# An early small inverse for the first token block of an S4 + GEGLU kernel, with half-size transposes and a new instruction list

## The chip, the cores and the metric

The kernel runs on one core of a Trainium2 chip. The time is device microseconds of one execution; before the change the median of three runs is 804.17 us (801.27 to 805.13). The core has five engines with an instruction stream each: TensorE (PE in the profile, with its weight loads as PEld), VectorE (DVE), ScalarE (ACT), GpSimd (POOL) and SyncE (SP). DMA transfers are issued from the streams of SP, ACT and POOL, and wait there in line with the engine's other instructions.

## What is computed

One sequence of 2048 tokens with 448 channels goes through two residual parts, both with a layer norm whose scale and shift come from a condition vector (adaLN).

```python
mod = silu(c) @ w_mod                       # six rows of 448: sa, ca, ga, sb, cb, gb
h = layernorm(x) * (1 + ca) + sa
K[d, l] = Re( sum_n C[d,n] * exp(dt[d] * A[d,n] * l) * dt[d] * B[d,n] )   # 448 x 2048, n = 256
y = irfft(rfft(h, 4096) * rfft(K, 4096))[:2048] + h * Dskip               # long convolution
x = x + ga * y
h = layernorm(x) * (1 + cb) + sb
x = x + gb * ((gelu(h @ w_gate) * (h @ w_up)) @ w_down)                   # 448 -> 1792 -> 448
```

The convolution is done in fp32, the two wide products of the second part with each fp32 operand split into two fp16 halves ("hi" and "lo").

## The kernel before

**Stage 1, generation and convolution.** The convolution kernel K is made on the chip. For each of 56 sets of eight channels ScalarE computes exponentials (L655, L637), angles go through TensorE (L668) and become sines and cosines on ScalarE (L681, L692, under one table load or another), VectorE multiplies them to tx and ty (L714, L718), and TensorE contracts over n (kgen, L741: 32 columns wide, in four column groups; then L764). Meanwhile the input is normalised and transformed. The transform of length 4096 is split in a stage over 32 and a stage over 128 rows; the results of the first stage go through DRAM and come back with other rows on the partitions. Channels come in three groups of 160, 160 and 128 (`GCH`). A group's transform runs over batches of frequencies: forward (TensorE), product with the input's transform (VectorE), inverse (TensorE), copy out of PSUM, store to `y_d` in DRAM.

**The join of the stages.** The last group's K is ready last, so its transform, `t_fft`, stands between the stages. It has nine batches (`TB`): eight of four frequencies and one of one. A batch is `t.fwd` (L1160), one product over 128 partitions (`t.p0`, L1166) and two over 64 (`t.p1`, L1169), `t.inv` (L1176, weights of 128 columns, all 2048 tokens), `t.z` (the copy out of PSUM, L473 on ACT or L475 on DVE, into one of two buffers "zo" or two "lh") and `t.st` (the store, L1184). PSUM for `t.inv` comes from the pool `fft` with two banks. Then the tokens of the first block (512 of 2048) are read back: `yi.l` (L1246, two per batch), and for the batch of one frequency `yi.d` (L1258, rows straight from zo to yi).

With yi complete, the second inverse stage runs for the first block: `co.mme` (L1356, the 320 channels of groups 0 and 1) can go early, `co.mml` (L1361, the last 128 channels) waits for all of yi. Then come the residual add, the statistics (L1368), the norm (L1403, L1404), the split into hi and lo (`hl`), the transposes `co.ta` (four of hi) and `co.tb` (four of lo, L1419) into one PSUM tile of eight, and the copies `co.ca`, `co.cb` into `ht`. The weights of the gate and up products are loaded and split by `w.hi` (L1297, ACT) and `w.lo` (L1301, DVE). Between these steps TensorE runs 18 "spins" (L1021), two matmuls each, whose result nobody reads.

**Stage 2, GLU.** For each of four blocks: gate and up (`gu2` and `gu`, L1470, L1476), gelu on ACT (L1483), product on DVE (L1490), split, and the product with w_down (L1576). The later blocks' loads and joins run beside it.

**What sets the order.** Nothing is ordered at run time. `PLACE` gives each step (by name and running number) a position in one list, and by a letter the engine or queue where there is a choice (a ScalarE, d VectorE, p POOL, s SP); `Plan.run` calls the steps sorted by that position, and so each engine's stream is written. The framework puts in the waits. Steps named `ev.` close pools of buffers, so that others can open on their memory; what is allocated there waits for the closed ones (`GATE`).

Of the kernel before, what the change touches and what calls it, by code (L numbers as in the profile page):

```python
# [40 lines left out]
    "anc": "106 134 153 161 146 178 189 230 255 295 302 329 320 337 428 447 456 478 486 512 502 561 568 617 660 684 694 687",  # L41
    "ang": "105 119 133 142 143 176 188 199 242 294 301 313 316 328 400 424 449 453 472 496 498 549 567 593 649 658 670 686 "
        "735 737 744 757 758 788 789 863 871 888 891 907 920 921 985 1000 1002 1014 1027 1033 1103 1111 1125 1127 1141 1150 "
        "1160 1172",
    "bn": "52 66 64 65 26 33 28 27 216 221 219 220 138 217 149 140",
    "c.ai": "1243",
    "c.ak": "174",
    "c.au": "17",
    "c.c": "8",
    "c.ea": "18",  # L50
    "c.ih": "1270",
    "c.ld": "6",
    "c.rd": "61",
    "c.t1": "19",
    "co.adde": "1310 1320 1338 1334",
    "co.addl": "1349 1354 1385 1388",
    "co.addx": "1469 1478 1479 1471 1647 1701 1674 1665 1766 1767 1781 1779",
    "co.c2": "1549d 1557d 1550d 1555a 1717d 1731a 1724a 1732d 1854a 1859d 1867a 1866a",
    "co.ca": "1378a 1379d 1414d 1415a",
    "co.cb": "1381a 1383d 1418a 1417a",  # L60
    "co.h0": "1364a 1371a 1400a 1403a",
    "co.h2": "1502d 1545a 1513a 1530d 1709a 1719a 1706a 1722d 1811d 1802a 1852d 1832a",
    "co.l0": "1372 1377 1406 1407",
    "co.l2": "1503 1547 1518 1541 1710 1720 1708 1723 1812 1804 1860 1853",
    "co.mme": "1303 1312 1314 1333",
    "co.mml": "1348 1353 1366 1374",
    "co.mmx": "1450 1473 1474 1451 1621 1695 1658 1620 1765 1746 1778 1777",
    "co.n": "1363 1369 1392 1397",
    "co.nx": "1492 1519 1508 1529 1707 1716 1704 1721 1810 1790 1793 1784",
    "co.rc": "1362 1368 1391 1393",  # L70
    "co.rcx": "1487 1703 1783",
    "co.rt": "1350 1355 1386 1390",
    "co.rtx": "1483 1702 1782",
    "co.t2": "1516 1556 1533 1551 1713 1725 1712 1727 1813 1847 1862 1855",
    "co.ta": "1365 1375 1408 1410",
    "co.tb": "1376 1382 1409 1411",
    "cos": "743 762 763 774 785 795 805 876 897 900 906 918 946 945 996 1009 1023 1040 1041 1048 1115 1121 1134 1155 1168 "
        "1169 1191 1207",
    "cos2": "118 135 154 162 152 187 193 238 260 297 304 335 323 340 436 448 459 483 487 516 507 564 573 621 675 685 701 693",
    "d.hi": "1524 1504 1544 1454 1486 1559 1468",  # L80
    "d.ld": "1511 1495 1532 1441 1481 1548 1456",
    "d.lo": "1528 1507 1546 1458 1488 1563 1472",
    "d0": "1",
    "dn": "1564 1565 1575 1576",
    "dn.k0": "1698 1849 1957",
    "dn.k2": "1711 1856 1959",
    "dn.k3": "1718 1861 1962",
    "dn.r": "1566 1568 1589 1578",
    "dn.r1": "1715 1872 1960",
    "dn.r4": "1728 1864 1964",  # L90
    "dn.r5": "1734 1871 1971",
    "dn.r6": "1735 1870",
    "dn.rh": "1965 1973 1977",
    "dn.s0": "1976",
    "dn.s1": "1978",
    "dn.st": "1573 1587 1617 1607 1748 1749 1750 1751 1972 1970 1898 1924 1969 1974 1975",
    "dn0": "1696 1697 1846 1848 1954 1955",
    "dn1": "1699 1850 1956",
    "dn2": "1726 1863 1966",
    "dn3": "1733 1865",  # L100
    "dn3h": "1967 1968",
    "dn4": "1705 1857 1961",
    "dn5": "1700 1851 1958",
    "dn6": "1714 1858 1963",
    "dsk": "34",
    "dt": "23",
    "e.f": "1618 1680 1661 1574 1610 1586 1639",
    "e.hi": "1623 1682 1662 1577 1611 1591 1645",
    "e.ld": "1613 1677 1650 1572 1609 1585 1626",
    "e.lo": "1624 1683 1667 1579 1615 1595 1648",  # L110
    "ev.end": "1229",
    "ev.fp": "691",
    "ev.geg": "1339",
    "ev.ps": "1313",
    "ev.ub": "380",
    "f.fc": "703 704 755 772 791 810 835 866 881 913 927 1003 1022 1034 1058 1083 1104 1124 1156 1173",
    "f.fwd": "729 754 771 797 818 847 868 893 908 935 959 981 993 1020 1039 1063 1084 1109 1126 1147 1179 1190",
    "f.inv": "738 765 786 809 832 857 874 902 923 949 968 991 1010 1032 1057 1069 1097 1123 1131 1161 1203 1215",
    "f.pr": "730 761 778 808 819 848 869 896 912 948 961 989 1005 1026 1042 1064 1089 1112 1128 1151 1181 1198",
    "f.st": "768 821 804 834 865 880 885 931 956 999 997 1006 1038 1078 1079 1094 1113 1143 1166 1201 1211 1222",  # L120
    "f.ut": "692 746 756 784 792 824 845 877 884 916 928 957 982 1004 1024 1035 1077 1085 1107 1132 1157 1174",
    "f.z": "747a 799a 790a 829a 861a 879a 883a 929a 947d 964a 986d 998d 1028a 1047a 1062a 1092d 1106d 1135a 1165a 1185a "
# [1657 lines left out]
```

## Time and profile before

| | before |
|---|---|
| median of three runs | 804.17 us (801.27 to 805.13) |
| profiled execution | 805.04 us |
| its span | 803.2 us |
| granted TensorE clock, mean | 0.987 |
| DMA | 136.72 MB, 170 GB/s over the span |
| chain that ended last | PE 73%, ACT 13%, DMA 5%, DVE 4%, issue 2% |

The span runs from the first to the last instruction. A row of busy time names the line of the kernel, the engine, the operation and the tiles (out<-in), then count, busy time, mean duration in ns and the idle time ahead of the group with what ended it. The chain is followed backwards from the last instruction: at each step to what released it. The profile's lines L... are those of the kernel before; in the changed kernel the same code stands 5 to 36 lines lower.

### The profile page before, as it was taken

The page shows a single profiled execution, that of the slowest core. Times are in us where ns is not written, and L with a number is a line of the kernel's source. Part 1 is how long each engine was busy: PE and PEld are TensorE (multiplying, and loading weights), DVE is VectorE, ACT ScalarE, POOL GpSimd, SP SyncE. Part 2 cuts the span into 40 slices and gives each one's busy share as a digit, 9 for nine tenths or more (in the row PEclk, how much of TensorE's full clock was granted, in tenths as well). Part 3 has the DMA queues.
Part 4 walks back from the last instruction along what each step waited for, and adds up shares of the span by engine and source line. Part 5 has one row for each costly group of instructions (what it writes and reads, how often), then busy time and mean ns, then how long its engine had stood idle before and what let it go on. Part 6 is the DMA issues. An engine that isn't in the chain of part 4 may idle for free.

```text
span 803.2 us, 19013 instructions
## 1 busy us (share of the span) xinstructions
PE 743.2 (93%) x8202; PEld 451.0 (56%) x8202; DVE 597.6 (74%) x896; ACT 456.7 (57%) x592; POOL 9.7 (1%) x25
## 2 busy tenths in 40 slices
PE   2677888999899999989899999999999999999998
PEld 1234444544577777769474445444595446954478
DVE  4889998999899999988667972288773776236462
ACT  3699999899899998951355730043441343113230
POOL 0000000000000000001200000000000000000000
PEclk9989999999999999999999999999999999999999
DMA  8554368898778857989587756246443222012101
GB/s 267 157 151 152 95 178 255 251 277 241 199 218 263 235 166 215 291 294 307 167 256 237 242 182 183 51 145 228 134 93 119 92 93 92 1 58 92 58 10 61
DMA packets 90397, 136.72 MB, mean 170 GB/s; under 512 B 21560, under 2 KB 72056, under 8 KB 90314
## 3 DMA queue, kind: packets, MB, share of 16 engines
q1 hardware_dynamic: 85808, 128.26, 53.3%
q10 hardware_dynamic: 3946, 6.60, 2.4%
q8 instruction: 64, 1.05, 0.5%
q0 software_dynamic: 560, 0.66, 0.3%
q14 instruction: 19, 0.16, 0.1%
HBM read 100.37 MB, written 36.01 MB: 170 GB/s over the span
## 4 chain that ended last, share of the span: by engine, by line
PE 73%; ACT 13%; DMA 5%; DVE 4%; issue 2%; SPq 0%; ACTq 0%; DVEq 0%; POOLq 0%
PE pq L1476 31%; PE pq L1576 9%; PE kg L741 4%; PE pg L668 4%; PE pd L1545 4%; PE pf L1089 4%; ACT my L655 2%; ACT fg L681 2%; PE pq L1470 2%; PE pf L970 2%; PE kg L764 2%; PE pf L1078 2%; ACT fg L692 2%; PE pd L1576 2%; DMA y<-zo 1%
## 5 line engine op out<-in xcount | busy, mean ns | idle before, releaser
L1476 PE MATMUL pq<-ht,wr 128*128 128x512 f16 (+1 forms) x1200 | 249.0, 365 | 1.7 <-DVE ht L475 0.9
L1476 PEld LDWEIGHTS <-wr 128*128 128x128 f16 x1200 | 114.5, 98 | 129.5 <-issue 13.2
L718 DVE TENSOR_TENSOR ty<-my,fg 128x2048 f32<-128x2048 f32 x56 | 127.4, 2285 | 1.0 <-ACT fg L692 0.5
L1483 ACT ACTIVATE ge<-pq 128x512 f32<-128x512 f32 (+1 forms) x60 | 33.8, 566 | 97.2 <-PE pq L1470 61.7
L1502 ACT ACTIVATE hh<-fq 128x1024 f16<-128x1024 f32 (+1 forms) x49 | 46.6, 963 | 72.6 <-DVE fq L1497 40.5
L1490 DVE TENSOR_TENSOR fq<-ge,pq 128x512 f32<-128x512 f32 (+1 forms) x60 | 39.0, 649 | 59.7 <-PE pq L1476 36.2
L1576 PE MATMUL pq<-d,hh 128*128 128x224 f16 x476 | 69.2, 259 | 0.0
L714 DVE TENSOR_TENSOR tx<-mx,fg 128x1024 f32<-128x1024 f32 x56 | 67.8, 1218 | 0.5 <-issue 0.5
L1505 DVE TENSOR_TENSOR hlo<-fq,hh 128x1024 f16<-128x1024 f32 (+1 forms) x49 | 53.7, 1106 | 18.4 <-ACT hh L1502 18.4
L741 PEld LDWEIGHTS kg<-ty,tx 128*32 128x32 f32 x3584 | 55.1, 113 | 20.8 <-issue 9.1
L741 PE MATMUL kg<-ty,tx 128*32 128x64 f32 x3584 | 64.4, 225 | 1.9 <-DVE tx L714 1.5
L1576 PE MATMUL pq<-d,hlo 128*128 128x224 f16 x238 | 61.6, 259 | 0.0
L681 ACT ACTIVATE fg<-pg 128x1024 f32<-128x1024 f32 x56 | 57.4, 1033 | 1.5 <-PE pg L668 1.0
L655 ACT ACTIVATE my<-pg 128x1024 f32<-128x1024 f32 x56 | 55.7, 1032 | 3.3 <-PE pg L650 2.9
L1576 PEld LDWEIGHTS <-hh 128*128 128x128 f16 x560 | 53.9, 98 | 0.6 <-issue 0.2
L1089 PE MATMUL pf<-q,fc 128*128 128x160 f32 x264 | 41.9, 308 | 1.3 <-DVE q L1082 0.9
L668 PEld LDWEIGHTS <-lt 64*128 64x128 bf16 x336 | 19.5, 95 | 42.1 <-issue 28.5
L668 PE MATMUL pg<-ea,lt 64*128 64x512 bf16 x168 | 34.5, 392 | 7.9 <-ACT fg L681 3.6
L1089 PEld LDWEIGHTS pf<-q,fc 128*128 128x128 f32 x264 | 36.5, 190 | 7.2 <-issue 4.4
L1693 ACT ACTIVATE d<-fq 128x896 f16<-128x896 f32 x14 | 13.2, 946 | 43.3 <-PE pd L1545 27.3
L668 PE MATMUL pg<-rd,lt 64*128 64x512 bf16 x168 | 34.0, 385 | 0.0
L668 PE MATMUL pg<-ea,rd 64*128 64x512 bf16 x168 | 34.0, 385 | 0.0
(191 smaller groups left out, 1139.9 us busy)
## 6 DMA issues: line engine op xcount, KB each, us to landing
wr<-w_d SPq DMA_DIRECT2D x21, 896.0 KB
fc<-in_k_fc SPq DMA_DIRECT2D x20, 576.0 KB
u_d<-so SPq DMA_DIRECT2D x32, 224.0 KB
ui<-u_d SPq DMA_DIRECT2D x10, 672.0 KB
fq<-in_wd SPq DMA_DIRECT2D x14, 448.0 KB
w<-in_wgu SPq DMA_DIRECT2D x11, 512.0 KB
us<-uo SPq DMA_DIRECT2D x22, 240.0 KB
q<-us SPq DMA_DIRECT2D x22, 240.0 KB
```

The lines of the kernel that those rows point to most:

```text
L655: A.activation(yb.tile.rearrange("p h (n k) -> p n h k", n=2), pb.tile.rearrange("p (n h k) -> p n h k", n=2, h=2), AF.Exp)
L668: T.matmul(pa[:, nh * 512:nh * 512 + 512], w, x, start=(k == 0), stop=(k == 2))
L681: A.activation(fb.tile[:, 0].rearrange("p x (n k) -> p n x k", n=2), pb.tile.rearrange("p (n x k) -> p n x k", n=2, x=2), AF.Sin, scale=TW ...
L714: V.tensor_mul(tx.tile, xb.tile[:, xm, None, :].to_broadcast([128, 2, 512]), fb.tile[:, :, 0])
L718: V.tensor_mul(ty.tile, yb.tile[:, :, None, :].to_broadcast([128, 2, 2, 512]), fb.tile[:, None, :, 1].to_broadcast([128, 2, 2, 512]))
L741: T.matmul(kg[32 * g:32 * g + 32, 2 * (s % 2) + q, :64], tx[:, r, nh, 4 * q + g], ty[:, 0:4:3, nh, 4 * q + g] if r else ty[:, 1:3, nh, 4 * ...
L1089: T.matmul(pz.tile[:, e % 32 - sl0], fc.tile[:, i, 1 + t], pp.tile[:, t, i], start=(t == 0 and e != 32), stop=(t == 1 and e != 0))
L1476: T.matmul(pb.tile[k][:, ts], wr.tile[:, 4 * lo + t, k, c0:c0 + 128], ht[:, m, ts], start=f % 2 == 0 and i == 0, stop=f % 2 == 1 and i == 9)
L1490: V.tensor_mul(to if half is None else to[:, half:half + 1], *src)
L1502: A.activation(hg.tile[0][:, cb, c], fq.tile[:, c], AF.Copy)
L1505: V.tensor_sub(hg.tile[1][:, cb, c], fq.tile[:, c], hg.tile[0][:, cb, c])
L1576: T.matmul(bank(k)[:, m], x[:, p, q[0], ts], w[:, p, q[1]], start=new and m == 0 and p == 0 and z == 0, skip_group_check=True, stop=i in ( ...
```

## The change

**A small inverse.** The columns of the inverse matrices are permuted so that the rows of a result come in order of token block. `t.i0` computes, from the same products, the inverse for the first block's tokens alone: 32 columns per frequency, the four frequencies of a batch in the four column groups of TensorE (`tile_position`). `t.z0` copies the 128 x 128 result into a buffer of the same two pairs "zo" and "lh", `t.s0` stores it (64 KB) into a new DRAM buffer `yb_d`, and `yi.l` reads the first block from there, two loads for each of the nine batches. `yi.d` is gone. The full `t.inv`, `t.z` and `t.st` stay: blocks 1 to 3 need them.

**Pools.** Products of the last five batches lie in the slots "my". The pool for norm, split and transposed tiles (`w0`) opens once the last batch's forward transform, the first two full inverses and the stores of group 1 are done, and PSUM for `co.mme` on the later token tiles and for the spins (`ev.pq`) once all products are done, not all copies.

**Half tiles.** For the first block, hi and lo are transposed into two PSUM tiles of four, from the pool `pd`; `co.ca` depends on the first four transposes alone.

**Spins.** 6 in place of 18.

**The list.** All of `PLACE` is new, in stage 1 as well, with other choices of engine in places.

```diff
-    spin(18, [EV["ps"], c_ih], Buf("pq"), None, lambda: POOLS["ps"].tile([128, 512], FT, name="pq0"),
+    spin(6, [EV["pq"], c_ih], Buf("pq"), None, lambda: POOLS["ps"].tile([128, 512], FT, name="pq0"),
...
+    perm = np.arange(128).reshape(2, 2, 2, 4, 4).transpose(3, 0, 1, 2, 4).reshape(128)
...
-        fc[:, i, 1] = c1.reshape(128, 128)
-        fc[:, i, 2] = c2.reshape(128, 128)
+        fc[:, i, 1] = c1.reshape(128, 128)[:, perm]
+        fc[:, i, 2] = c2.reshape(128, 128)[:, perm]
...
-    y_d = [dram.tile([32, 2, 64, n], FT, name="y%d" % g) for g, n in enumerate(GCH)]
+    y_d = [dram.tile([32, 128, n], FT, name="y%d" % g) for g, n in enumerate(GCH)]
+    yb_d = dram.tile([32, 2, 2, 2, 4, 128], FT, name="yb_d")
...
+        def inv0():
+            p0.tile = fft.tile([128, 128], FT, name="pf")
+            for t in range(2):
+                for i, (b, k, _) in enumerate(fs):
+                    e = EORD[i0 + i]
+                    r = 32 * (e % 32 - sl0)
+                    T.matmul(p0.tile[r:r + 32], b.tile[:, k, 1 + t, :32], pp.tile[:, t, i],
+                             start=(t == 0 and e != 32), stop=(t == 1 and e != 0), tile_position=(0, r))
+
+        def zout0(e):
+            z0.tile = pq.tile([128, 128], FT, name=z0.tag, bufs=2)
+            cp(e, z0.tile[:32 * ns], p0.tile[:32 * ns])
+
+        def store0(q):
+            QF[q](yb_d[sl0:sl0 + ns].rearrange("s r h g j d -> (s r h g j) d"), z0.tile[:32 * ns])
...
+        t5 = add("t.i0", {"PE": 0.52 if ne > 1 else 0.25}, v, inv0, t4, [p0], fb + [pp])
+        t6 = add("t.z0", {"ACT": 0.2, "DVE": 0.2}, v, zout0, [t5], [z0], [p0])
+        S0[bi] = add("t.s0", {"SP": 0.41, "ACT": 0.4, "POOL": 0.83}, v, store0, [t6], (), [z0], kb=16 * ns)
...
+            def yl(q, s0=s0, ns=ns, g=g):
+                QF[q](y_rows(YI[0].tile, 2)[64 * g + 2 * s0:64 * g + 2 * (s0 + ns)],
+                      yb_d[s0:s0 + ns, :, :, g].rearrange("s r h j d -> (s r) h (j d)"))
+            YL.append(add("yi.l%d" % g, {"SP": 0.68, "ACT": 0.75, "POOL": 0.7}, 58.5 + 0.1 * bi, yl, [S0[bi], t_yi], (),
+                          [YI[0]], kb=16 * ns))
...
-    EV["ps"] = add("ev.ps", {"NONE": 0.0}, 58.9, ev_ps, TZ + MR)
+    EV["pq"] = add("ev.pq", {"NONE": 0.0}, 58.8, ev_pq, TQ)
+    EV["ps"] = add("ev.ps", {"NONE": 0.0}, 58.9, ev_ps, TZ + MR + [EV["pq"]])
+    EV["w0"] = add("ev.w0", {"NONE": 0.0}, 58.8, ev_w0, [YO[1, b] for b in range(NB)] + [TI[0], TI[1], TS[len(TB) - 1]])
...
-            def tr16(k0=None, pt=pt, hl=hl):
-                if not k0:
-                    pt.tile = POOLS["ps"].tile([128, 8, 128], HF, name="pt")
-                for k in range(k0 or 0, 8 if k0 is None else k0 + 4):
-                    T.transpose(pt.tile[:, k], hl.tile[:, 128 * k:128 * k + 128], K2["ih"])
+            pts = [pt, pt if blk else Buf("pd")]
+
+            def tr16(k0=None, pts=pts, hl=hl):
+                b = pts[1 if k0 else 0]
+                n, k0 = (8, 0) if k0 is None else (4, k0)
+                b.tile = POOLS["pd" if n == 4 else "pt"].tile([128, n, 128], HF, name="pd" if n == 4 else "pt")
+                for k in range(n):
+                    T.transpose(b.tile[:, k], hl.tile[:, 128 * (k0 + k):128 * (k0 + k) + 128], K2["ih"])
```

Two lines of the table show its form, those of the spins:

```diff
-    "spin": "1325 1335 1336 1342 1343 1344 1345 1346 1347 1352 1356 1357 1358 1359 1360 1361 1367 1373",
+    "spin": "1312 1320 1321 1332 1333 1376",
```

What it does to the streams is seen at three places. The first is TensorE ahead of the join. Before (L1176 is the full inverse, L1356 the join's early channels, L1021 a spin; the join's last channels, L1361, come after sixteen spin matmuls more):

```order
L1160 MATMUL pf<-ako,my 128x128 x6
L1176 MATMUL pf<-q,fg 128x128 x32
L1356 MATMUL pd<-yi,ai 64x320 x2
L1176 MATMUL pf<-q,fg 128x128 x4
L1176 MATMUL pf<-q,my 128x128 x12
L1356 MATMUL pd<-yi,ai 64x320 x2
L1356 MATMUL pq_5259<-yi,ai 64x320 x2
L1021 LDWEIGHTS idenh
L1021 MATMUL pq_5278<-idenh 128x512
```

Now (L1195 is the small inverse, L1186 the full one, L1381 and L1386 the join's early and last channels, L1447 the transposes), from the last spin matmul ahead of the join on:

```order
L1026 MATMUL pq_5264<-idenh 128x512
L1186 MATMUL pf<-q,fg 128x128 x8
L1381 MATMUL pq_5261<-yi,ai 64x320 x2
L1186 MATMUL pf<-my,fg 128x128 x16
L1386 MATMUL pd<-yi,ai 64x128 x4
L1186 MATMUL pf<-my,fg 128x128 x12
L1186 MATMUL pf<-my 128x128 x4
L1447 LDWEIGHTS hl
```

All full inverses stood ahead of the join, the last two with the early channels between; now three of the later batches stand close ahead of it, two behind it, and the last one ahead of the first GLU matmul. The small inverses stand before all of this, two to eight rows of matmuls each.

The second place is POOL's queue from the first store of the last group on. Before:

```order
L1184 DMA y_69<-zo 128x3x128
L1258 DMA yi<-zo 1x4x128 x2
L1246 DMA yi<-y_69 8x2x512 x2
L1258 DMA yi<-zo 1x4x128 x2
L1246 DMA yi<-y_69 6x2x512
L1246 DMA yi<-y_69 8x2x512
L1258 DMA yi<-zo 1x4x128 x2
L1246 DMA yi<-y_69 8x2x512 x3
```

Now (L1203 is the small store, L1275 the load of the first block, L1210 the full store):

```order
L1203 DMA yb_d<-zo 128x128
L1203 DMA yb_d<-lh 96x128
L1203 DMA yb_d<-lh 32x128
L1203 DMA yb_d<-zo 128x128
L1275 DMA yi<-yb_d 8x2x512
L1275 DMA yi<-yb_d 6x2x512
L1275 DMA yi<-yb_d 8x2x512 x2
L1275 DMA yi<-yb_d 6x2x512
L1203 DMA yb_d<-zo 128x128
L1275 DMA yi<-yb_d 8x2x512 x6
L1210 DMA y_69<-lh 128x4x128
L1210 DMA y_69<-zo 128x4x128 x3
```

The queue had one store and loads; now it has five small stores among the loads, and full stores at its end.

The third place is the start, on ScalarE, from the last step that takes the time step dt to the copy zo for the modulation. Before:

```order
L554 ACTIVATE q<-q,dts__105 112x256
L588 DMA lh_d<-lh 112x1536
L573 ACT_TABLE_LOAD
L573 ACTIVATE q<-q 112x256
L581 ACTIVATE q<-q 112x256
L826 ACTIVATE rows<-pf 128x448
L473 ACTIVATE zo<-pf 128x448
```

Now:

```order
L559 ACTIVATE q<-q,dts__106 112x256
L790 ACTIVATE sig<-c_sb 112x4
L478 ACTIVATE lh<-q 112x2x256 x2
L578 ACT_TABLE_LOAD
L578 ACTIVATE q<-q 112x256
L593 DMA lh_d<-lh 112x1536
L586 ACTIVATE q<-q 112x256
L478 ACTIVATE zo<-pf 128x448
```

Two casts (L478 into lh) that VectorE did stand on ScalarE, the table load and the store come after them, and the copy zo stands ahead of the rows of the modulation.

More of the change, by code (lines that the diff above doesn't have):

```diff
@@ L428, in s4_geglu @@
     V.memset(eps, 1e-5)
-    ph1, ph1b, ph1t, ph1f = (ExitStack() for _ in range(4))
+    ph1, ph1b, ph1t, ph1f, ph1c = (ExitStack() for _ in range(5))
     cst = ph1.enter_context(tc.tile_pool(name="cst", bufs=1))
@@ L437, in s4_geglu @@
     pq = ph1b.enter_context(tc.tile_pool(name="pq", bufs=4, side="right", reuse_waits="tile"))
-    akps = [ph1b.enter_context(tc.tile_pool(name="ak0", bufs=1, side="right"))]
+    akps = [ph1c.enter_context(tc.tile_pool(name="ak0", bufs=1, side="right"))]
     uas, gzs = ExitStack(), ExitStack()
@@ L1031, in s4_geglu @@
     X1, W = {}, {}
-    yv = [y.rearrange("s r (h g j) d -> (s r) g h (j d)", h=2, g=2) for y in y_d]
+    yv = [y.rearrange("s (b r h g j) d -> s b r g h (j d)", b=4, r=2, h=2, g=2) for y in y_d]
     def y_rows(t, c):
```

111 lines of the change are left out of this document (53 added, 58 removed), and 433 rows, old and new, of the table PLACE.

## The prediction

> **What bounds the kernel now.** I read the busy shares first, then busy time by stretch, then the chain that ended last around the change of stage, and last the single groups on it.
>
> ```profile
> PE 743.2 (93%) x8202; PEld 451.0 (56%) x8202; DVE 597.6 (74%) x896; ACT 456.7 (57%) x592; POOL 9.7 (1%) x25
> ```
>
> A share of 93% is a mean over two stages. By stretch (columns: stretch, length, busy PE, PEld, DVE, ACT, POOL, granted clock, DMA share):
>
> ```profile
> 0.00:40.00 40.00, 17.89 (x64) 7.70 (x65) 26.76 (x63) 21.01 (x32) 1.55 (x11) 0.96 0.74 212
> 40.00:361.00 321.00, 291.70 (x5278) 183.21 (x5278) 301.40 (x350) 295.01 (x360) 0.00 (x0) 0.98 0.75 217
> 320.00:361.00 41.00, 36.69 (x863) 28.44 (x863) 38.19 (x39) 31.94 (x38) 0.00 (x0) 1.00 0.92 288
> ...
> 361.00:382.00 21.00, 20.98 (x181) 20.18 (x182) 18.07 (x29) 4.24 (x7) 2.77 (x5) 1.00 0.99 304
> ...
> 404.00:800.00 396.00, 394.61 (x2574) 231.03 (x2573) 235.27 (x419) 129.06 (x182) 0.00 (x0) 1.00 0.39 123
> ```
>
> From 404 to 800 us only TensorE counts (394.6 of 396): nothing there gets shorter without fewer matmuls, and the change leaves that stage's matmuls as they are. From 40 to 361 three engines are each over 90% busy, so their order decides. Between lies the join of the stages, 361 to 404.3, which is a chain (start, length, what):
>
> ```profile
> 357.12 1.10 PE kg L741 x64
> ...
> 361.00 3.14 PE pf L1160 x26
> ...
> 372.99 3.59 PE pf L1176 x32
> ...
> 376.65 0.61 ACT zo L473
> ...
> 377.27 4.17 DMA y<-zo
> ...
> 381.53 0.61 ACT zo L473
> ...
> 382.15 2.50 DMA y<-zo
> ...
> 384.94 0.69 DVE zo L475
> ...
> 385.66 0.41 DVE x L1367
> 386.07 4.22 DMA y<-zo
> ...
> 390.89 2.29 DMA yi<-y
> ...
> 393.95 0.44 PE pd L1361 x4
> ...
> 395.30 4.38 PE pq L1021 x12
> ...
> 400.27 0.97 PE pq L1021 x4
> ...
> 402.80 0.95 ACT wr L1297
> ...
> 404.28 1.80 PE pq L1476 x15
> ```
>
> I call 361.00, the first forward transform of the last group, T0. The last load lands so late that the last group's join (L1361) starts at T0+32.95; the GLU matmuls run from T0+43.3, or T0+42.85 if the four that ran a little earlier are taken off. What stands between the last product (VectorE) and the join is three copies and three stores in a row, because two zo buffers are used over and over:
>
> ```profile
> 379.46 1.39 DVE L1169 TENSOR_TENSOR q<-my,pf 64x512 f32<-64x512 f32 x2
> ...
> 384.94 0.69 DVE L475 COPY zo<-pf 128x512 f32<-128x512 f32 x1 [4.09 <-DMA y<-zo]
> ```
>
> The last product ends at 380.85 = T0+19.85, and a copy then sits 4.09 us behind a store.
>
> **The change, part by part.** (1) *Small inverse.* A transform whose weights are 32 columns wide, four in four column groups, has its like in L741: 64 matmuls of 64 columns in 1.10 us, 17 ns each. With 128 columns 34 ns; the 66 written ones run as two passes (L1160 shows 66 records for 33 written), so 132 × 34 ns = 4.5 us more TensorE. Twelve spins go, 24 matmuls at 0.24 us (0.97 for four) = 5.8 us. These spins filled waiting time, and the small inverse runs while the products bound: I cost both at nothing. Without the column groups running together it would be 132 × 0.121 (3.14/26) = 16 us.
>
> (2) *The products* (VectorE, 0.69 us each) keep their number. Two small copies are put among them and one full copy of the first batch more than before:
>
> ```profile
> L475 DVE COPY zo<-pf 128x128 f32<-128x128 f32 x1 | 0.3, 292 | 0.0
> ```
>
> 2 × 0.29 + about 0.45 = +1.0: last product at T0+20.85.
>
> (3) *From there to the join.* The shortest data path: small inverse 0.5, copy 0.3, issue and landing of the store 0.4 + 2.5, load 2.29 with 0.65 + 0.78 around it (the gaps before and after the load at 390.89): T0+28.3. But TensorE's order puts four spins (1.9), three full inverses (3.59/2 = 1.8 each) and a join matmul group (0.4) behind the last small inverse and ahead of the join: 20.85 + 0.5 + 1.9 + 5.4 + 0.4 = T0+29.1 at the earliest. These inverses also need PSUM banks that copies empty, and copies need buffers that stores empty: nine small and four full copies go through four buffers before, three turns each. A store from the POOL queue, which gets four of the first five small stores, is shown once, and its loads beside it:
>
> ```profile
> y<-zo POOLq DMA_DIRECT2D x1, 192.0 KB, 8.1
> ...
> yi<-y POOLq DMA_DIRECT2D x6, 32.0 KB, 3.4
> ```
>
> At 3.4 us a turn is about 4.4, three turns 13, from the first copy at T0+6 to T0+19: not binding. At 8.1 a turn is 9.2, so T0+33.7, and one inverse more: T0+35.5. I take T0+32: 64 KB is nearer in size to the 32 KB, but the stretch has a DMA share of 0.99. Against 32.95 that is −0.95, with ends −3.85 (T0+29.1) and +2.55 (T0+35.5). The Trainium skill ("DMA: Bandwidth & Descriptors", section on the SWDGE path) gives a POOL transfer as about 2.0 us plus its bytes at 436 GB/s, an estimate of 2.15 us for 64 KB; by that the order of TensorE alone would bind, and the sum would be 2.9 us lower. The trace speaks against it: 192 KB took 8.1 us, where the page makes 2.45.
>
> *Its queues.* The eight tiny DMAs from zo straight to yi go (six on POOL, two on SP), nine small stores come (five on POOL, two each on SP and ScalarE's queue), and the full stores now stand behind the loads. POOL issues 16 DMAs before the join, at up to
>
> ```profile
> 367.10 0.79 POOL L1184 DMA_DIRECT2D y<-zo  x1 [364.79 <-ACT zo L473]
> ```
>
> each, 12.6 us of the 26 from T0+6 on: room enough. But a load that waits on POOL for its store holds the next small store behind it; that is one more reason not to take T0+29.1. On SP the third weight load stands ahead of the last stores where it stood behind them, so the cast that follows it is sooner free.
>
> (4) *From the join to the GLU* it took 42.85 − 32.95 = 9.9 us, most of it statistics, normalisation, transposes. The half tiles let a copy begin after four transposes, not eight; against that the last full inverse, 1.8 us, now stands ahead of the first GLU matmul, in the place where TensorE waits for a weight cast (L1297, 402.80) and a copy until 404.28, about 1.8 us after its transposes; if the copies come sooner, the inverse does not. I take 9.7: −0.2, between −1 and +1.
>
> (5) *Where spins go, the clock may.* In the last column but two:
>
> ```profile
> 395.00:396.00 1.00, 1.00 (x7) 0.43 (x6) 0.84 (x5) 0.29 (x1) 0.00 (x0) 0.73 0.00 0
> 396.00:397.00 1.00, 1.00 (x4) 0.32 (x3) 0.96 (x4) 0.30 (x1) 0.00 (x0) 0.50 0.43 102
> ...
> 398.00:399.00 1.00, 1.00 (x4) 0.42 (x3) 0.96 (x3) 0.35 (x3) 0.00 (x0) 0.56 0.73 299
> 399.00:400.00 1.00, 1.00 (x12) 0.57 (x9) 0.97 (x3) 0.67 (x2) 0.00 (x0) 1.00 1.08 444
> ```
>
> TensorE had stood for 2.6 us before 393.95; 1.3 us later it got half its clock for 3.3 us, which hit only spins. Now the gap between the join and the transposes (5.7 us before, full of spins) holds one join and two inverses, 4 us, so gaps stay near 2 us: cost 0, at most 1.65 (3.3 us at half clock under the first GLU matmuls). The Trainium skill ("TensorE: Matmul & The Clock Gate", Part 1) wants an idle window of about 3.4 us for that; by that rule the cost is 0 as well, but here 2.6 us was enough.
>
> (6) *Phase 1.* At the start one product of the modulation is taken ahead, and both halves of another run in one go:
>
> ```profile
> 15.35 5.55 PE L808 MATMUL pf<-fg,c_sb 112*128 112x448 f32 x8 [15.35 <-DMA fg<-in_w_mod]
> ...
> 26.25 4.87 PE L808 MATMUL pf<-fg,c_sb 112*128 112x448 f32 x8
> ...
> 24.74 0.54 ACT L473 ACTIVATE zo<-pf 128x448 f32<-128x448 f32 x1
> ...
> 33.00 2.86 ACT L655 ACTIVATE my<-pg 128x1024 f32<-128x1024 f32 x3
> ```
>
> The copy zo can move from 24.74 to about 20.8 (a table load, two casts and three small steps ahead of it); then 0.5 + 10.4 gives 31.7 where the second half now ends at 31.1, so the first exponential moves from 33.0 to 33.6: +0.6. Six casts change from VectorE to ScalarE, and two table loads go:
>
> ```profile
> L473 ACT ACTIVATE lh<-q 112x512 bf16<-112x512 f32 x6 | 3.8, 630 | 1.2 <-DVE q L529 1.1
> L573 ACT ACT_TABLE_LOAD x1 | 1.3, 1283 | 5.5 <-DVE q L566 5.5
> ...
> L475 DVE CAST lh<-q 112x512 bf16<-112x512 f32 x10 | 4.2, 425 | 1.0 <-ACT q L554 0.7
> ```
>
> VectorE 6 × 0.425 = −2.6; ScalarE 6 × 0.63 − 2 × 1.28 = +1.2; the other copies that change sides come to −0.5 and +1.2 by the same count. VectorE ends the stage (38.19 of the last 41 us), ScalarE has 26 us idle there against 19.6: I take half of −3.1, and with the start T0 comes 1.0 us earlier. What the new order opens or closes of idle no row shows; a quarter of VectorE's 19.6 us either way is 4.9, so −6 to +5.5.
>
> (7) The stage from 404 on: its first load of block 1 comes later but has tens of microseconds; 0, within 1.
>
> Sum: −1.0 − 0.95 − 0.2 = −2.15. The profiled execution took 805.04 (span 803.2), close to the slowest of the three runs shown; on the median of 804.17 the forecast is 802.0.
>
> **Rivals.** *A, the chain gives all it could.* Stores land in 2.2 to 3.4 us, the join comes at T0+29.1: −1.0 − 3.85 − 0.2 gives 799.1. For it: HW-queue stores of 256 KB took 2.50 beside traffic. Against: 4.17, 4.22 and 8.1 in the same stretch. The skill's price for a POOL transfer leads here.
>
> *B, slower: ScalarE becomes what phase 1 waits for.* It gets 2.4 us more work and keeps copies that wait for TensorE in its own queue:
>
> ```profile
> ACT ke L473 <- PE kg L741: 4.8, 2, 4.0
> ```
>
> Exponentials, angles and cosines stand behind such a copy, TensorE's angle matmuls behind these, VectorE's products behind all. Two more waits of 4.0 us make 802.0 + 8.0 = 810.0; from one and a half on the kernel is slower than can be told from none (0.5%, 4.0 us, about what a measurement of this kernel can tell from no change). For it: the order is new through all 361 us. Against: ScalarE's idle, 26 us, would absorb a part.
>
> *C, the clock.* Gaps of over 2.6 us between join and GLU bring half clock: 802.0 + 1.65 = 803.7; the gain is then hardly to be seen.
>
> **How the numbers follow.** Forecast 0.42 (own range 799.5 to 805.5), A 0.28, B 0.22, C 0.08. Faster by over 0.5% (under 800.1): 0.25 of A and 0.13 of the forecast's low side, 0.38. Slower (over 808.2): 0.24, B and a little of the rest. Within: 0.38. The range goes from 795 (A with a phase 1 that loses 4 us of idle) to 810, the middle of B.
>
> **What would show it.** T0 in the new trace, against 361.0, tells the phase 1 step (360.0 expected; over 366 is B). The last product at T0+20.85, the join at T0+32 and the first GLU matmul 9.7 us later tell steps 2 to 4; a small store on POOL that lands in under 3 us speaks for A, over 8 against my T0+32. The granted clock between join and GLU tells 5: spins and gaps there, and half clock in the GLU, are C. Wrong I would be above all by phase 1, whose idle I could only bound.

## The result, and the profile after

The changed kernel takes 814.53 us (median of 4 runs, 812.34 to 815.19), the kernel before 803.72 us (4 runs, 801.27 to 805.13): the ratio is 1.0133, with a 95% interval of 1.0101 to 1.0165. It is 10.8 us slower, where a gain of 2.15 us, to 802.0, was forecast, and lies above the range's end of 810. (The ratios here and below are not the quotients of the two medians, and differ from them a little.)

The profiled execution took 814.39 us with a span of 812.6, 9.4 more than the span before. The marks that the prediction named show where (in us, each stage by itself; the first GLU matmul is taken as the first one that starts):

| stage | before | forecast | after |
|---|---|---|---|
| start to T0 (first forward transform of the last group) | 361.0 | 360.0 | 361.3 |
| T0 to the end of the last product | 19.85 | 20.85 | 26.85 |
| last product to the join of the last channels | 13.1 | 11.15 | 13.8 |
| join to the first GLU matmul | 8.9 | 8.7 (0.2 less) | 8.9 |
| first GLU matmul to the last matmul | 396.6 | 396.6 | 397.7 |
| rest | 3.7 | 3.7 | 4.0 |

Seven of the 9.4 us are lost among the products, where the forecast had put a price of 1.0 us and no wait. The same stretches of time as before (columns as in the prediction):

```profile
361.00:382.00 21.00, 16.76 (x150) 14.97 (x154) 12.49 (x23) 1.15 (x3) 3.33 (x6) 0.84 0.65 192
382.00:400.00 18.00, 15.00 (x152) 9.38 (x143) 12.17 (x21) 3.17 (x7) 5.51 (x10) 0.91 0.53 162
400.00:411.00 11.00, 10.84 (x102) 9.30 (x102) 10.30 (x26) 7.54 (x14) 2.29 (x3) 1.00 0.60 174
411.00:800.00 389.00, 387.11 (x2488) 222.46 (x2487) 230.22 (x410) 125.88 (x178) 1.50 (x2) 1.00 0.39 125
```

From 361 to 382 TensorE was busy all the time before (20.98 of 21); now it is 16.8, VectorE 12.5 in place of 18.1, and the clock 0.84 in place of 1.00, with the DMA engines at 0.65 in place of 0.99. The chain through that stretch:

```profile
367.69 0.30 DVE zo L480
...
368.29 6.69 DMA yb_d<-zo
...
375.14 0.29 ACT zo L478
...
375.47 4.63 PE pf L1186 x20
380.10 1.66 PE pf L1168 x8
...
385.01 0.29 ACT zo L478
...
385.31 5.97 DMA yb_d<-zo
...
391.31 0.29 ACT zo L478
...
391.64 0.96 PE pf L1195 x16
...
398.22 3.77 PE pf L1186 x32
401.99 0.39 PE pd L1386 x4
```

(Columns: start, length, engine or DMA, tile, line.) This is read so: a small copy by VectorE fills a zo buffer; its store (64 KB, issued by POOL) takes 6.69 us to land; only then may ScalarE's copy into the same buffer run; that copy (of another small inverse) empties the PSUM bank for a full inverse (L1186), and behind that inverse stands a forward transform (L1168) that the next product needs. A copy waits a second time, for a store issued by ScalarE, 5.97 us; the products are over by then, and what stands behind it is the last small inverse (391.64) and with it the way to the join. ScalarE's row for the first of these copies, from the timeline of the changed kernel (in brackets the idle time before it and what ended it):

```profile
375.14 0.28 ACT L478 ACTIVATE zo<-pf 128x128 f32<-128x128 f32 x1 [4.30 <-DMA yb_d<-zo]
```

And VectorE's rows there, from the same timeline:

```profile
373.59 1.98 DVE L1179 TENSOR_TENSOR my<-my,pf 64x512 f32<-64x512 f32 x3
381.80 0.69 DVE L1176 TENSOR_TENSOR my<-my,pf 128x512 f32<-128x512 f32 x1 [6.23 <-PE pf L1168]
...
386.77 1.39 DVE L1179 TENSOR_TENSOR my<-my,pf 64x512 f32<-64x512 f32 x2
```

The copy waited 4.30 us for the store, the products 6.23 us for the forward transform. The two small stores that POOL issued next, at 371.12 (48 KB) and 373.27 (16 KB), landed within 1 us of the first one, after 4.6 and 2.7 us. TensorE in that place, from short stretches of the changed kernel (stretch, length, busy with its count, granted clock, DMA share, GB/s):

```profile
373.00:375.00 2.00, 0.00 (x0) 0.94 0.33 101
375.00:377.00 2.00, 1.53 (x7) 0.50 0.11 36
...
379.00:381.00 2.00, 2.00 (x12) 0.50 0.00 0
381.00:383.00 2.00, 2.00 (x26) 0.85 0.00 0
...
391.00:393.00 2.00, 1.36 (x18) 0.71 0.60 193
393.00:395.00 2.00, 2.00 (x6) 0.50 0.48 131
```

TensorE stood still from 372.7 to 375.5 and then ran at half its clock until 381.6: the twenty matmul records at 375.47 take 4.63 us, where they take 2.2 to 2.4 at full clock in the kernels below. Half clock came a second time, from 391.8 to 395.2, behind the second wait (TensorE idle for 2.13 us before 391.64). There the small inverse takes 0.96 us, where sixteen of its records took 0.57 ten us earlier, and eight spin matmuls take 3.15, where four took 0.97 at full clock in the kernel before: some 1.6 us more on the way to the join.

### The profile page after: what moved, and what is told of

It reads as the page before. It is cut to its first block, busy times and chain, and to the rows that moved or that the text cites. A ratio compares the mean times of both kernels' runs of the same rounds, so it can differ in the third digit from the quotient of the medians.

```text
span 812.6 us, 19253 instructions
## 1 busy us (share of the span) xinstructions
PE 747.5 (92%) x8310; PEld 454.0 (56%) x8310; DVE 597.5 (74%) x896; ACT 455.5 (56%) x599; POOL 14.2 (2%) x32
## 3 DMA queue, kind: packets, MB, share of 16 engines
q0 software_dynamic: 992, 2.15, 0.9%
## 4 chain that ended last, share of the span: by engine, by line
PE 51%; DMA 2%; DVE 1%; issue 0%; ACT 0%; ACTq 0%
PE pq L1504 30%; PE pq L1604 8%; PE pd L1573 4%; PE pq L1498 2%; DMA yb_d<-zo 2%; PE pd L1604 1%; PE pf L1186 1%; PE pd L1381 1%; PE pt L1447 1%; PE pf L1168 0%; PE pq L1026 0%; PE pd L1386 0%; PE pf L1195 0%; PE pd L1664 0%; PE pq L1664 0%; DVE ht L480 0%
## 5 line engine op out<-in xcount | busy, mean ns | idle before, releaser
L746 PE MATMUL kg<-ty,tx 128*32 128x64 f32 x3584 | 62.4, 223 | 1.9 <-ACT ako L478 0.7
L673 PEld LDWEIGHTS <-lt 64*128 64x128 bf16 x336 | 19.7, 95 | 47.1 <-issue 32.7
L1094 PE MATMUL pf<-q,fc 128*128 128x160 f32 x264 | 41.9, 308 | 1.7 <-DVE q L1087 1.7
L769 PE MATMUL kg<-ak,ke 128*64 128x128 f32 x448 | 31.2, 279 | 2.8 <-issue 2.8
L673 PE MATMUL pg<-rd,lt 64*128 64x512 bf16 x168 | 33.6, 391 | 0.0
```

Of the source, the lines that this page charges most:

```text
L673: T.matmul(pa[:, nh * 512:nh * 512 + 512], w, x, start=(k == 0), stop=(k == 2))
L746: T.matmul(kg[32 * g:32 * g + 32, 2 * (s % 2) + q, :64], tx[:, r, nh, 4 * q + g], ty[:, 0:4:3, nh, 4 * q + g] if r else ty[:, 1:3, nh, 4 * ...
L1094: T.matmul(pz.tile[:, e % 32 - sl0], fc.tile[:, i, 1 + t], pp.tile[:, t, i], start=(t == 0 and e != 32), stop=(t == 1 and e != 0))
```

## The experiments

Four theories were to be told apart, with rivals that the expectations name. **S**: a small copy waits for a buffer until an earlier small store has landed. **Q**: the store is late because POOL issues it. **L**: it is late because of the bytes of big loads that were issued ahead of it. **C**: the standstill costs a second time through the clock. The marks of all kernels, in us from their own T0 (each from one profiled execution; that of e_buf was the slowest of its ten):

| kernel | last product | join | first GLU matmul | time against the kernel before (95%) |
|---|---|---|---|---|
| before | 19.9 | 33.0 | 41.9 | |
| after | 26.9 | 40.6 | 49.5 | 1.0133 (1.0101 to 1.0165) |
| e_buf | 22.0 | 32.7 | 41.6 | 1.0001 (0.9975 to 1.0026) |
| e_queue | 22.1 | 35.8 | 44.7 | 1.0068 (1.0043 to 1.0093) |
| e_load | 27.0 | 40.5 | 49.4 | 1.0102 (1.0044 to 1.0160) |
| e_clock | 24.5 | 38.8 | 47.5 | 1.0093 (1.0058 to 1.0128) |
| e_ql | 23.9 | 38.2 | 47.1 | 1.0095 (1.0060 to 1.0129) |
| e_bufw | 21.1 | 31.0 | 39.9 | 1.0037 (1.0016 to 1.0058) |
| v2 | 21.1 | 29.8 | 38.8 | 0.9985 (0.9966 to 1.0004) |
| v3 | 21.1 | 30.8 | 39.7 | 1.0001 (0.9981 to 1.0021) |
| v4 | 21.1 | 29.7 | 38.6 | 0.9980 (0.9960 to 1.0000) |
| b_spin6 | 19.8 | 33.6 | 42.4 | 1.0002 (0.9985 to 1.0018) |

### Buffers of their own for the small copies (e_buf)

A tile of its own for each of the nine small copies; all else as in the changed kernel:

```diff
-        p0, z0 = Buf("pf"), Buf("zo" if bi % 2 else "lh")
+        p0, z0 = Buf("pf"), Buf("z0")
...
-            z0.tile = pq.tile([128, 128], FT, name=z0.tag, bufs=2)
+            if "z0" not in POOLS:
+                POOLS["z0"] = POOLS["wp"].tile([128, 9, 128], FT, name="wr")
+            z0.tile = POOLS["z0"][:, bi]
```

> The changed kernel, with the nine small copies going into a scratch tile of their own (a slot of the weight buffers that is free at that time), so that no small copy waits for a store; order, queues, spins stay. Theory S (a copy waits for a buffer until a small store has landed, TensorE behind it, the products behind TensorE): the wait of 4.3 us of the copy on ScalarE and the 2.8 us gap of TensorE at T0+11 go, the products run through to about T0+21, the last-channel join starts at T0+30 to T0+33 instead of T0+40.6, the time falls by 7 to 10 us, to about 805 to 807. Rival Q (it is the POOL queue's slowness on the way of the data, not the buffers): the loads still land late, the join at T0+37 or later, at most 3 us gained. Rival G (the loss is in other stages): no change.

No small copy waits for a store any more, the products go through to T0+22.0, and the loss is gone within the noise: the time is that of the kernel before (medians 806.08 and 804.41 us, ratio 1.0001, 0.9975 to 1.0026). Order, queues and spins are those of the changed kernel, so S holds; G, its rival there, falls, and so does Q as the cause of the loss, since POOL still issues the same stores. With the standstills the half clock behind them goes too, so this run does not part S from C. In the chain of e_buf stand the same inverses (the twenty records now take 2.43) and a store and a load of the data:

```profile
375.32 2.43 PE pf L1186 x20
...
382.14 7.22 DMA yb_d<-wr
...
392.67 2.87 DMA yi<-yb_d
...
395.79 0.45 PE pd L1388 x4
```

A small store still takes 7.22 us, now on the way of the data to the join, and the early inverse gains nothing: T0+32.7 for the join, 33.0 before. This execution also began the last group at half clock, as that of e_clock below did (stretch of e_buf, TensorE's columns):

```profile
361.00:367.00 6.00, 5.22 (x29) 0.50 0.98 381
```

So its last product, about 1 us later than in the kernels that come after (T0+22.0 against 21.1), is late for that reason too.

### The small stores off the POOL queue (e_queue)

```diff
-    "t.s0": "1271p 1258p 1276p 1277p 1287s 1291a 1316s 1334p 1338a",
+    "t.s0": "1271a 1258s 1276a 1277s 1287s 1291a 1316s 1334a 1338a",
```

> The changed kernel, with the five small stores of the POOL queue issued by SP and ScalarE instead; buffers and all positions stay. Rival Q (the software queue makes the store land late): the first small store lands in 2 to 3 us instead of 6.7, the gap of TensorE at T0+11 goes, 5 us or more gained. Rival L (the bytes of the big loads issued just before lie ahead of it in the DMA engines): the first small store still takes 5 us or more, gain under 2 us, or a loss.

The issues of the first two small stores on SP's queue in e_queue (one row; the first starts at its head), and after them ScalarE's copy into the buffer of the first, from its timeline:

```profile
367.20 7.69 SPq L1203 DMA_DIRECT2D yb_d<-zo  x2
```

```profile
374.26 0.28 ACT L478 ACTIVATE zo<-pf 128x128 f32<-128x128 f32 x1 [4.23 <-DMA yb_d<-lh]
```

By the kernel the copy waits for that store's buffer (the profile names another transfer that landed then; the trace's own count of landings has SP's store land at 374.10, and the small inverse to be copied was ready at 371.35). SP issued the store at 367.20, so the copy came 7.1 us after it, as late as from POOL (375.14 against 368.29, 6.9). Q falls for this store. The time fell all the same, by about half the loss. A part of that is a side effect: with the other letters the framework gave the second full inverse the PSUM bank that VectorE's copy empties, not the one that waits for ScalarE's, so TensorE stood for 0.4 us where it had stood for 2.8, and the clock stayed whole until 386. How the rest is split was not measured.

### The big loads later in the list (e_load)

```diff
-    "x1.ld": "1246 1455 1639 1784",
+    "x1.ld": "1285 1455 1639 1784",
...
-    "yi.e": "1256",
+    "yi.e": "1286",
```

> The changed kernel, with the load of the first block's x (896 KB) and the four early loads of yi (1.3 MB) issued some 15 us later on SP's queue, behind the first small stores; nothing else moved. Rival L: the first small store on POOL lands in 2 to 3 us instead of 6.7, the gap of TensorE at T0+11 shrinks to under 1 us, and as far as the loads are not late themselves for the join of the early channels, 3 to 6 us are gained. Rival Q: the store still takes over 5 us and nothing is gained; the moved loads may cost up to 4 us.

This told nothing on L: nothing stands on SP's queue between the old place and the new one that waits, so SP issued the loads at the same time as ever (timeline of SP's queue, e_load):

```profile
361.61 0.50 SPq L1243 DMA_DIRECT2D x<-in_A_u  x1
362.15 4.24 SPq L1266 DMA_DIRECT2D yi<-y  x4
```

The first small store took 6.84 us, and everything else came as in the changed kernel.

### The big loads behind the first small store (e_ql)

Against e_queue:

```diff
-    "x1.ld": "1246 1455 1639 1784",
+    "x1.ld": "1259 1455 1639 1784",
...
-    "yi.e": "1256",
+    "yi.e": "1259",
```

> The kernel of e_queue (small stores on SP's and ScalarE's queues), with the load of the first block's x (896 KB) and the four early loads of yi (1.3 MB) put on SP's queue right behind the first small store, so that they cannot be issued before it. In e_queue ScalarE's copy into the same buffer began 7.1 us after the first small store was issued. Theory L (bytes of loads issued earlier lie ahead of the store): that copy begins within 3 to 4 us of the issue, the first full inverse of the later ones no longer waits, and 1 to 4 us come off, unless the loads of yi are then late for the early channels. Rival M (a small store takes 6 to 7 us there whatever lies ahead): the copy begins 6 us or more after it, no gain.

SP's queue in e_ql, the first small store and then the loads:

```profile
366.27 0.33 SPq L1203 DMA_DIRECT2D yb_d<-zo  x1
366.64 2.55 SPq L1266 DMA_DIRECT2D yi<-y  x4
```

POOL's load of what that store wrote, and ScalarE's copy into that store's buffer, from the timeline of e_ql:

```profile
368.71 0.57 POOL L1275 DMA_DIRECT2D yi<-yb_d  x1 [366.43 <-DMA yb_d<-zo]
...
370.48 0.28 ACT L478 ACTIVATE zo<-pf 128x128 f32<-128x128 f32 x1 [1.39 <-DMA yi<-y]
```

The copy comes 4.2 us after the store's issue (370.48 against 366.27), where it was 7.1, and the store is not what it waits for: the small inverse that it copies ends on TensorE at 370.41. The store itself had landed before POOL's load, which waits for it, was issued at 368.71; by the trace it took 1.5 us from issue to landing, where it took 6.7 in the changed kernel. The next small store, issued at 369.13 behind the four loads of yi (1.3 MB; the load of x, 896 KB, was issued 0.1 us after it), takes the time over, in the chain of e_ql:

```profile
369.13 6.67 DMA yb_d<-lh
```

So L holds for both: with the 2.2 MB issued behind it, the first store lands about 5 us sooner; a store behind the loads of yi takes 6.7. M falls, since the store's time changed with what lay ahead of it. The sum is no gain against e_queue (1.0095 against 1.0068): ScalarE's next copy into an "lh" buffer now waits 5.1 us for the second store, TensorE stands still for 2.3 us behind it, and the clock is at half from 377.1 to 380.5.

### The gap filled with dummy matmuls (e_clock)

```diff
+    spin(6, [EV["end"], c_ih], Buf("pd"), None, lambda: POOLS["pd"].tile([128, 512], FT, name="pd"),
+         lambda t: (K2["ih"], K2["ih"][:, None].to_broadcast([128, 4, 128]), t.rearrange("p (a b) -> p a b", b=128)))
...
-    "spin": "1312 1320 1321 1332 1333 1376",
+    "spin": "1272 1272 1272 1272 1272 1272 1312 1320 1321 1332 1333 1376",
```

> The changed kernel, with twelve dummy matmuls (2.9 us at full clock) put on TensorE just ahead of the full inverse that waits 2.8 us at T0+11, so that TensorE does not stand still there; nothing else. Theory C (the gap costs twice, once as a wait and once more as half clock from 375 to 382): the granted clock stays at 1.00 in that stretch, the 6.9 us of work there take 3.5 to 4, the products come 3 us sooner, and the join comes at T0+37 to T0+38.5: 2 to 3.5 us gained. If the clock costs nothing because other waits fill in, the join stays at T0+40 and the time the same within 1 us.

The chain of e_clock in the gap:

```profile
374.76 2.70 PE pd L1026 x12
377.46 2.23 PE pf L1186 x20
```

The dummies run in the gap, and the same twenty records take 2.23 us in place of 4.63. The last product comes 2.4 us sooner after T0, the first GLU matmul 2.0 us. So C holds as to direction, and this first stretch of half clock is worth about 2 us of the 7.7 lost between T0 and the GLU. That is rather too little: the dummies run on after the store has landed (375.97), and the full inverse begins 0.8 us later after T0 than in the changed kernel. The second stretch of half clock is still there (from 391.6 to 395.1). In the measured time (1.0093 against 1.0133) the two intervals overlap, so on the clock's share the trace carries more than the times. The wait for the store (S) is not changed by this edit: the last product is still 3.4 us behind that of e_bufw below, where it is gone (0.8 of it by the dummies).

### Weight loads earlier (e_bufw)

Against e_buf:

```diff
-    "w.le": "1289 1319 1288",
+    "w.le": "1257 1257 1257",
```

> The kernel of e_buf (scratch tile for the small copies), with the three early weight loads (512 KB each) issued right behind the early loads of yi instead of 15 to 20 us later. In e_buf a small store that was issued just behind two of these loads took 7.2 us to land, and the join hung on it. Theory L: no small store after T0+15 takes over 3 us, the join starts at T0+28 to T0+30.5 instead of T0+32.7, 2 to 4 us come off against e_buf. Rival M: the stores keep their 7 us, no gain.

Small stores from the POOL queue in e_bufw, from the DMA issues of two stretches (KB each, median us from issue to landing):

```profile
yb_d<-wr POOLq DMA_DIRECT2D x2, 64.0 KB, 6.8
```

```profile
yb_d<-wr POOLq DMA_DIRECT2D x1, 64.0 KB, 2.3
```

The first row is of 365 to 376 and the median of two stores: one issued at 368.21, behind the loads of x and yi and the first of the weight loads, took 8.0 us, one issued at 373.69, behind all three, 5.6. The second row is of 380 to 390 (a store at 383.36), with no large load issued for 11 us: 2.3 us for the same 64 KB from the same queue. The DMA engines were busy for a share of 1.05 in the first stretch and 0.40 in the second. The late ones harm nobody, since no copy waits for them, and the last ones are quick. The join comes at T0+31.0, 1.7 us sooner than in e_buf, of which up to 0.9 is e_buf's late products; T0+28 to T0+30.5 was expected. TensorE has no gap from 382.4 on, and nothing waits for a load at the join: TensorE's own order binds there.

In the times nothing shows: 806.14 us, ratio 1.0037 (1.0016 to 1.0058), slower than the kernel before by a little, though its join comes 2 us sooner. Four of its ten runs took 808.8 to 809.4 us and six 804.7 to 806.3; the one that was profiled is a quick one, so what the slow four lose is not known.

### Towards a better version (v2, v3, v4)

v2, against e_bufw:

```diff
-    "spin": "1312 1320 1321 1332 1333 1376",
+    "spin": "1312 1376",
...
-    "t.s0": "1271p 1258p 1276p 1277p 1287s 1291a 1316s 1334p 1338a",
+    "t.s0": "1271p 1258p 1276p 1277p 1287s 1291a 1316s 1334a 1338a",
...
-    "yi.l0": "1304p 1299s 1322s 1328s 1345p 1339a 1346p 1351p 1349a",
+    "yi.l0": "1304p 1299s 1322s 1328s 1345s 1339a 1346p 1351s 1349a",
...
-    spin(6, [EV["pq"], c_ih], Buf("pq"), None, lambda: POOLS["ps"].tile([128, 512], FT, name="pq0"),
+    spin(2, [EV["pq"], c_ih], Buf("pq"), None, lambda: POOLS["ps"].tile([128, 512], FT, name="pq0"),
```

> e_bufw with two more edits: one small store and two loads at the end taken off the POOL queue (to ScalarE and SP), and two spins instead of six, so that TensorE has 1.9 us less in front of the join. If the join hangs on the data, the queues give up to 1 us more; if it hangs on TensorE's order, the spins give up to 1.9 us. Join at T0+27 to T0+29.5, time 1.5 to 4 us under that of the kernel before (800 to 802.5). If the clock falls in a new gap it is up to 1.7 us more.

The join comes at T0+29.8, a little behind the T0+27 to T0+29.5 that was expected, and the first GLU matmul at T0+38.8, 3.1 us sooner than in the kernel before. TensorE's rows in the timeline of v2 show what binds now:

```profile
384.13 2.05 PE L1186 MATMUL pf<-q,fg 128*128 128x128 f32 x16 [0.41 <-DVE wr L480]
...
386.81 3.84 PE L1186 MATMUL pf<-my,fg 128*128 128x128 f32 x32
390.57 0.66 PE L1388 MATMUL pd<-yi,ai 128*64 128x128 f32 x8
391.16 2.94 PE L1186 MATMUL pf<-my,fg 128*128 128x128 f32 x24
```

From 384.13 on TensorE has no gap: full inverses ahead of the join, behind it, and one more ahead of the GLU. Of the 3.1 us the times show 0.8 (802.89 against 803.72 us): the GLU stage is 1.1 us longer with the new list, as in the changed kernel, the profiled execution of the kernel before, 805.04 us, was itself 1.3 above the median here, and the ratio's interval (0.9966 to 1.0004) includes no change.

v3, against v2, drops the spins and puts one full inverse ahead of the last small ones:

```diff
-    spin(2, [EV["pq"], c_ih], Buf("pq"), None, lambda: POOLS["ps"].tile([128, 512], FT, name="pq0"),
-         lambda t: (K2["ih"], K2["ih"][:, None].to_broadcast([128, 4, 128]), t.rearrange("p (a b) -> p a b", b=128)))
...
-    "t.inv": "1259 1273 1274 1335 1337 1348 1366 1367 1393",
+    "t.inv": "1259 1273 1274 1312 1337 1348 1366 1367 1393",
```

> The kernel of v2 with no spins at all and one full inverse (the fourth) put ahead of the last small ones, into the time in which TensorE waits for the last product. In v2 TensorE runs without a gap from T0+23.4 to the first GLU matmul, so its own order is the bound there: 1.1 us of spins and about 1 us of idle time can go, the first GLU matmul comes at T0+36.5 to T0+38 (38.8 in v2, 41.9 in the kernel before), the time 1 to 2 us under v2 and 2 to 3.5 us under the kernel before. If the data are the bound by then, or TensorE falls to half clock, nothing is gained on v2.

The chain of v3:

```profile
382.63 1.98 PE pf L1186 x16
384.62 0.62 PE pf L1195 x16
...
385.58 2.22 DMA yb_d<-wr
...
388.57 2.40 DMA yi<-yb_d
...
391.53 0.45 PE pd L1388 x4
```

That missed: the inverse (1.98) now stands ahead of the last small one, and the data are the bound: small inverse, copy, store 2.22, load 2.40. v4 takes the inverse back; against v3:

```diff
-    "t.inv": "1259 1273 1274 1312 1337 1348 1366 1367 1393",
+    "t.inv": "1259 1273 1274 1335 1337 1348 1366 1367 1393",
```

> The kernel of v2 with no spins, the fourth full inverse back in its place behind the last small inverse. In v3 the data came last: the inverse ahead of the last small one delayed that by 2.0 us. Here the small inverse is not delayed: the join starts at T0+28.8 to T0+29.4 by the data path of v3 less 2.0, or by TensorE's order of v2 less 0.5 to 1.1; first GLU matmul at T0+37.7 to T0+38.4, the time up to 1 us under v2, 1 to 3 us under the kernel before. If gaps bring half clock into the GLU it is 1 to 2 us more.

The join comes at T0+29.7 and the first GLU matmul at T0+38.6, both 0.2 to 0.3 us behind the late end of what was expected; the time is 803.31 against 804.66 us, ratio 0.9980 (0.9960 to 1.0000). That is the lowest ratio of the study, not to be told from v2's 0.9985, and its interval just touches one: no kernel here is faster than the one before beyond doubt.

### Six spins in the kernel before (b_spin6)

```diff
-    "spin": "1325 1335 1336 1342 1343 1344 1345 1346 1347 1352 1356 1357 1358 1359 1360 1361 1367 1373",
+    "spin": "1325 1335 1336 1342 1343 1373",
-    spin(18, [EV["ps"], c_ih], Buf("pq"), None, lambda: POOLS["ps"].tile([128, 512], FT, name="pq0"),
+    spin(6, [EV["ps"], c_ih], Buf("pq"), None, lambda: POOLS["ps"].tile([128, 512], FT, name="pq0"),
```

> The kernel before with six spins instead of eighteen, nothing else changed. If the spins only fill waiting time (step 5 of the prediction with the clock unharmed): the same time within 1 us. If TensorE's clock falls because of the missing spins: half clock somewhere between 391 and 408, up to 1.7 us slower.

TensorE by short stretches in b_spin6:

```profile
392.00:394.00 2.00, 0.00 (x0) 0.61 0.05 18
394.00:396.00 2.00, 1.12 (x8) 0.50 0.04 8
...
400.00:402.00 2.00, 2.00 (x13) 0.50 0.54 219
402.00:404.00 2.00, 1.41 (x11) 0.83 0.00 0
```

Both halves came in part: the clock is at half from 392.4 to 402.7, and the time is the same (1.0002). The work in that stretch, join and transposes, waits mostly for VectorE's norm, and the clock is back when the GLU begins.

## Why the prediction was wrong, point by point

**Small inverse (1)**: its size was right. Sixteen records of it take 0.57 us, so 132 take 4.7 where 4.5 was worked out. That it costs nothing came true only where no small copy waits for a store (products at T0+21.1 in e_bufw and v2 to v4); in the changed kernel, where TensorE and not VectorE held up the products, groups of it stand on the chain.

**The products (2)** is the step that failed. It let them run through to T0+20.85, "the small inverse runs while the products bound"; they ended at T0+26.85. It gave this step no ends either, so the range could not cover the loss. The forward transforms that feed them stand in TensorE's list behind full inverses whose bank a copy must empty, and that copy waited for a store. With that wait taken away (e_buf, e_bufw, v2 to v4) they end at T0+21.1 to T0+22.0, near what was worked out.

**From there to the join (3)**: the mechanism was named here (copies through four buffers, a turn per store), but it was applied to the inverses in front of the join and not to the forward transforms, and so its worst case ended at T0+35.5. The join came at T0+40.6. The choice of T0+32 rested on a landing time between 3.4 and 8.1 us; the small stores in that stretch took 6.69 and 5.97, nearer to the row for 192 KB, which is to say that the size was not what decided. The shortest path of the data, T0+28.3, was about right: v3, less the 2.0 us that it lost, has it at T0+28.8. TensorE's order, T0+29.1 at the earliest, was not: e_bufw has that order, runs it without a gap and comes to T0+31.0. Of the 1.9 us between, 1.2 are a group of the early channels and a spin that stand ahead of the last small inverse and that the sum left out. That v2 and v4 come to 29.8 and 29.7 is no confirmation, since they have four and six spins fewer.

The price that the Trainium skill ("DMA: Bandwidth & Descriptors", SWDGE path) gives for a POOL transfer, 2.15 us for 64 KB by estimate, about holds in these traces where no large load lies ahead (2.3 us in e_bufw, 1.8 in the changed kernel at 375.70), and not in the busy stretch (5.6 and 8.0 in e_bufw, 6.7 in the changed kernel). Rival A, which it led, fell.

**From the join to the GLU (4)**: by the first matmul it is 8.9 us before and after. By the prediction's own mark, which takes off the four matmuls that ran early before (T0+42.85), it is 9.9 before and 8.9 after: 1.0 us gained where 0.2 was forecast, at the end of its range. Whether the half tiles have a part in that is not shown, as no run has them alone; in v2 TensorE's own list (two full inverses, transposes, one more inverse) fills the stretch.

**The clock (5)** was costed at nothing and looked for at the wrong place. Half clock came ahead of the join, twice, each time behind a standstill that the forecast did not have: at T0+13.4 (2.8 us of standstill; e_clock puts its price at 2.0 to 2.4 us) and at T0+30.5 (2.13 us; some 1.6 us by the rows, and no run takes it away alone). In e_bufw and v2 to v4, where no small copy waits, the clock is whole from T0 to the last matmul. Where the forecast put C, between join and GLU, no half clock came in the changed kernel, and in b_spin6, where it came, it cost nothing that shows.

**Phase 1 (6)**: −1.0 was forecast, +0.3 came. The first exponential starts at 33.84 (33.6 forecast). Over the kernels with the new list T0 lies between 359.6 and 363.1 with hardly anything changed ahead of it, so that the new order of stage 1 can be called neither better nor worse. Rival B had the right sign for another reason, and its place shows nothing.

**The GLU stage (7)** is 1.1 us longer in the changed kernel and in v2 alike, where 0 within 1 was forecast. Waits of TensorE make 0.2 of it (1.72 and 1.90 us in all). The other 0.9 is TensorE's busy time there, 396.11 against 395.21 us; the 112 transposes of that stretch, for one, take 8.45 in place of 8.07. Why the same matmuls take longer in the new order is not shown.

## What to carry to other kernels

A step that is put ahead of others takes buffers too: count the copies that go through each buffer pair, put the store's landing into the turn, and follow the wait through PSUM to every instruction that stands behind it on TensorE, not only to the one that you want sooner. In these runs a small store was late by what had been issued ahead of it, on whatever queue; a buffer of its own for what must not wait took the loss away, while moving the big loads behind one store only moved the wait to the next. A standstill of TensorE can cost a second time through its clock. Moving a step in a list moves nothing in time if its queue has no wait between the two places.

## What the runs showed of the hardware

A 64 KB store from one queue took between 2.3 and 8.0 us in one kernel (e_bufw), by what had been issued ahead of it, and 1.5 us in e_ql with the DMA engines almost idle. With the loads ahead the issuing engine made no difference that shows (7.1 us from SP, 6.9 from POOL, from the issue of the same store to the copy behind it). TensorE's clock fell to half after a standstill of 2.8 us and stayed there for 6.8 us, 6.1 of them unbroken work; after one of 2.1 us it stayed there for 3.4, as it did in the kernel before after 2.6; in b_spin6, with work that comes and goes, for 10.2. The Trainium skill ("TensorE: Matmul & The Clock Gate", Part 1) gives an idle window of about 3.4 us for the fall, and as much busy time for the return; in these traces shorter gaps were enough, and half clock lasted one, two or three times 3.4 us.
